# Two batches of a packed attention and FFN kernel: float32 products over half of d_ff in place of three float32r products

## The chip, the cores and the metric

The kernel runs on one core of a Trainium2 chip. The metric is the device time of one execution in microseconds; the median of three runs stands for a kernel. A profiled execution is a run of its own: it gives the span from the first to the last instruction, which is a little shorter than the device time.

## The reference

Two attentions follow one another, and an FFN follows them. With batch 8, 8 heads, 576 tokens, head size 64 and 32 packing vectors per head:

```python
p_packed = sm_attn(p, k, v)               # 32 packed vectors per head
out = sm_attn(q, p_packed, p_packed)      # 576 tokens attend to the 32
x = out.transpose(0, 2, 1, 3).reshape(B * S, H * D)      # 4608 x 512
h = x @ w_in                              # 512 -> 2048
g = np.maximum(h, 0.0) + alpha * np.minimum(h, 0.0)
return g @ w_out                          # 2048 -> 512
```

`sm_attn` is the softmax attention with scale 1/8. The weights w_in and w_out come to the kernel as 64-bit floating point numbers, which it converts itself on ACT and DVE.

## The kernel before

**The algebra.** The second attention's output is its probabilities a (576 tokens by 32 columns for each of 8 heads, 256 in all) times the packed vectors. The kernel multiplies the packed vectors into w_in first, giving pw (256 x 2048 for each batch, in pieces `pw[b, j]` of 512 columns of d_ff, j = 0 to 3). The FFN's first product is then pw against a, with a contraction of 256, two blocks of 128.

**Precision.** A float32 operand x is used either whole, as float32, or split into two float32r parts, xh = round(x) on ACT and xl = x - xh on DVE or POOL. A product of two split operands is three float32r products (hh, hl, lh). A product of two whole operands is one float32 product in the program, and two weight loads and two matmul records in the trace.

**The FFN loop.** The loop runs over 256 steps (k, f): k is a half-batch of 288 tokens (k // 2 is the batch), f one of 16 blocks of 128 of d_ff. At each step `first(k, f)` (L619) computes the first product into the PSUM tile `ps_h` (two buffers), then the activation: `neg` on ACT (L646) and a multiply and add on DVE back into `ps_h` (L647). Then the result is split: `gh` on ACT (L652), `gl` on DVE (L653). `second(k, f)` (L656), two steps behind, multiplies gh and gl by the f-th block of w_out into four accumulators `acc`, twelve float32r products a step (L670 to L672). The order of the steps is written out by hand: with `sweep(b, f0)` going over both half-batches of b, it is batch 0 f 0 to 3, batch 0 f 4 to 7, batch 1 f 0 to 7 (steps 0 to 31); batch 0 f 8 to 11, batch 0 f 12 to 15, batch 1 f 8 to 15 (steps 32 to 63); then batches 2 to 7 one after the other, 32 steps each. The accumulators hold one sweep; partial sums of the first two batches go through tiles `part`.

**First product.** For batch 0 (k < 2 * XF, XF = 1) it is whole: L628, two float32 products, with pw and a unsplit. For the others `split_pw` (L607) splits a piece of pw (256 columns of d_ff at a time: `pwh` on ACT for k < 4, L613, `pwl` on DVE, L616), and L640 to L642 are six float32r products a step.

**What feeds the loop.** Generators, each advanced once or more a step by a plan (L759 to L769) of (first step, generator, every how many steps; negative: how many times a step):

- `convert` (L106) turns a 512-column piece of 64-bit weights into float32 on ACT (L121, L123) and DVE (L125 to L139), and, if the caller wants it split, makes the parts on ACT (L141) and DVE (L142). `convert_w_out(f)` (L159) does this for the 16 blocks of w_out, two of them ahead of the loop, the next from step 0 on.
- `packed_w_fine` and `packed_w_first` make pw of batch 0 for j = 0 and 1 from whole w_in, and store the whole pieces in DRAM as `w_whole`.
- `packed_w` (L562) makes pw from split w_in. With "whole" it loads a piece of `w_whole` (256 KB, L572), splits it (ACT L573, DVE L574) and stores the parts as `w_split` (512 KB, L579); with "fresh" it converts from the input; otherwise it loads `w_split` (512 KB, L568). Three float32r products of 512 columns follow (L596 to L598), and ACT copies the result to pw (L601). Before, batch 1 takes j = 0 and 1 by "whole" from step 7, batches 0 and 1 take j = 2 and 3 by "fresh", and the later pairs load `w_split`, batches 2 and 3 from step 53.
- `attention(b, tp)` (L229) makes a of one batch for half of its heads in some 15 advances. Batches 0 and 1 use float32 products in it (`exact`), L207, L212 and L347; the others split. For batch 0 the end is one DVE transpose (L444) into a whole tile; for the others a transpose (L454), a cast on ACT to `a_h` (L455) and a subtraction on POOL to `a_l` (L456). The tiles `a_h` and `a_l` have three buffers each.

All DMAs go through SP's queue, in order. Within each engine the order of instructions is fixed when the program is built.

Of the kernel before, what the change touches and what calls it, by code (L numbers as in the profile page):

```python
# [8 lines left out]
F32 = mybir.dt.float32  # L9
# [13 lines left out]
def fv(ap):  # L23

    return ap.bitcast(F32)
# [3 lines left out]
def pack_attention_ffn_kernel(  # L29
# [74 lines left out]
    XF = 1  # L104

    def convert(src, raw, place, whole=None, room=None):  # L106
# [32 lines left out]
        nc.vector.tensor_tensor(out=bits, in0=bits, in1=low, op=ALU.add)  # L139
        hi, lo = place()  # L140
        nc.scalar.copy(out=hi, in_=mag)  # L141
        nc.vector.tensor_tensor(out=lo, in0=mag, in1=fv(hi), op=ALU.subtract)  # L142

# [15 lines left out]
    def convert_w_out(f):  # L159
        def place():  # L160
            wo_t[f] = const.tile([P, 2, DM], F32R, name=f"wo{f}", tag=f"wo{f}")
            return wo_t[f][:, 0, :], wo_t[f][:, 1, :]

        return convert(w_out[f * P : (f + 1) * P, :], new_raw(f), place)
# [64 lines left out]
    def attention(b, tp, exact=False):  # L229
# [211 lines left out]
        if b < XF:  # L441
            if b not in result:
                result[b] = at.tile([P, 2, S], F32, name="a_f", tag="a_h")
            nc.vector.transpose(  # L444
                out=result[b][:, tp, :], in_=t1.rearrange("p g n -> p (g n)")
# [3 lines left out]
            split_pt()  # L449
# [9 lines left out]


# [100 lines left out]

    def packed_w(bs, units, source="split"):  # L562
# [55 lines left out]

    def first(k, f):  # L619
# [4 lines left out]
        if k < 2 * XF:  # L624
            th, a_f = pw[k // 2, f // 4], result[k // 2]
# [20 lines left out]
        nc.scalar.activation(out=neg, in_=x, func=AF.Relu, scale=-1.0)  # L646
        nc.vector.scalar_tensor_tensor(  # L647
# [8 lines left out]
    def second(k, f):  # L656
# [10 lines left out]
        gh, gl = gs.pop((k, f))  # L667
        for o in range(NOC):
            os_ = slice(o * P, o * P + P)
            nc.tensor.matmul(acc[o][:, :HS], wo_t[f][:, 0, os_], gh, start=begin, stop=False)  # L670
            nc.tensor.matmul(acc[o][:, :HS], wo_t[f][:, 1, os_], gh, start=False, stop=False)  # L671
            nc.tensor.matmul(acc[o][:, :HS], wo_t[f][:, 0, os_], gl, start=False, stop=end)  # L672
# [16 lines left out]

    result, pw, pj, gs, acc, part = {}, {}, {}, {}, [], {}  # L690
# [20 lines left out]
    def units(*js):  # L711
        return [(j, pr) for j in js for pr in range(NP)]

# [51 lines left out]
    plan += [(A2[4], packed_w([2, 3], units(*range(NJ))), 1)]  # L765
# [51 lines left out]
```

## Time and profile before

| what | us |
|---|---|
| median of 3 runs | 811.91 (811.84 to 813.56) |
| profiled execution, span | 809.3 |
| PE, matmul records busy | 773.0 (5376 records) |
| PE, weight loads busy | 729.5 |
| DVE busy | 605.8 |
| ACT busy | 497.1 |
| POOL busy | 191.4 |
| mean granted TensorE clock | 0.992 |

Busy time is the union of an engine's records. A matmul's record goes on past the time in which the next one can start, so PE's busy time is above what its products need; the pace of a run of products in the chain of waits, or in a window that holds nothing else, says what one of them takes. In the groups a row gives the line, engine, operation, output and inputs, shapes and count, then busy time and mean duration of one in ns, then the idle time before it and what ended it. In the chain of waits a row has start, duration and what ran.

### The profile page before, as it was taken

Reading aid. Unit: us, or ns where it says so; the run is one execution under the profiler, and the core shown is the slowest. Engines: PE = TensorE matmul, PEld = TensorE weight load, DVE = VectorE, ACT = ScalarE, POOL = GpSimd, SP = SyncE. Lnnn points to the kernel's source line nnn. Section 1 sums busy time; section 2 is a strip of 40 time slices with the busy share of each in tenths; the row PEclk is TensorE's granted clock in tenths of the full one; section 3 lists DMA queues with packets and bytes.
Section 4 is the critical chain, followed back from the end, with each engine's and each line's share of the span. In section 5 each row is a group of like instructions: output and inputs, shape, how many; then the busy total and the mean of one; then the engine's idle time right before and its main releaser. Section 6 shows DMA issues by size and latency. Waiting matters only on the chain.

```text
span 809.3 us, 14930 instructions
## 1 busy us (share of the span) xinstructions
PE 773.0 (96%) x5376; PEld 729.5 (90%) x5376; DVE 605.8 (75%) x1301; ACT 497.1 (61%) x1165; POOL 191.4 (24%) x195
## 2 busy tenths in 40 slices
PE   6779899999989899999999999999999999999997
PEld 4557688989989799999999999999999999999997
DVE  3998989877887656898896477987875566666664
ACT  4888798876767775665657756665567533333332
POOL 2101411235346212354342014534410000000000
PEclk9979999999999999999999999999999999999999
DMA  9976787422223843322216722311027000000000
GB/s 312 340 233 223 262 304 236 151 54 83 78 88 101 267 151 104 93 59 82 70 59 212 235 59 59 91 58 45 2 92 256 20 31 1 31 1 31 1 30 30
DMA packets 58457, 93.77 MB, mean 116 GB/s; under 512 B 5136, under 2 KB 36880, under 8 KB 58384
## 3 DMA queue, kind: packets, MB, share of 16 engines
q1 hardware_dynamic: 58384, 92.83, 35.7%
q8 instruction: 42, 0.69, 0.4%
q14 instruction: 31, 0.25, 0.1%
HBM read 72.88 MB, written 19.92 MB: 115 GB/s over the span
## 4 chain that ended last, share of the span: by engine, by line
PE 80%; DVE 8%; DMA 5%; ACT 5%; issue 1%; POOL 0%; SPq 0%; ACTq 0%; DVEq 0%
PE acc L670 15%; PE acc L671 15%; PE acc L672 15%; PE ps_h L640 7%; PE ps_h L641 7%; PE ps_h L642 7%; PE ps_h L628 3%; DMA vraw<-in_v 2%; PE ps_m L352 2%; PE ps_m L216 1%; PE ps_m L217 1%; PE ps_m L596 1%; PE ps_m L598 1%; PE ps_m L597 1%; DMA w<-w_split 1%
## 5 line engine op out<-in xcount | busy, mean ns | idle before, releaser
L670 PE MATMUL acc<-gh,wo 128*128 128x288 f32 x1024 | 286.2, 300 | 3.5 <-ACT gh L652 3.1
L671 PE MATMUL acc<-gh,wo 128*128 128x288 f32 x1024 | 281.8, 295 | 0.0
L670 PEld LDWEIGHTS acc<-gh,wo 128*128 128x128 f32 x1024 | 192.2, 188 | 9.8 <-ACT gh L652 5.6
L672 PE MATMUL acc<-gl,wo 128*128 128x288 f32 x1024 | 199.2, 299 | 0.0
L671 PEld LDWEIGHTS acc<-gh,wo 128*128 128x128 f32 x1024 | 192.4, 188 | 1.6 <-issue 0.2
L652 ACT CAST gh<-ps_h 128x288 fp32r<-128x288 f32 x256 | 101.6, 399 | 115.3 <-DVE ps_h L647 113.2
L646 ACT ACTIVATE neg<-ps_h 128x288 f32<-128x288 f32 x256 | 105.3, 412 | 107.2 <-PE ps_h L642 95.5
L653 DVE TENSOR_TENSOR gl<-ps_h,gh 128x288 fp32r<-128x288 f32 x256 | 115.2, 452 | 70.4 <-ACT gh L652 68.5
L647 DVE SCALAR_TENSOR_TENSOR ps_h<-neg,nal,ps_h 128x288 f32<-128x288 f32 x256 | 131.2, 515 | 47.2 <-ACT neg L646 46.5
L672 PEld LDWEIGHTS acc<-gl,wo 128*128 128x128 f32 x1024 | 157.4, 188 | 3.1 <-issue 0.4
L640 PE MATMUL ps_h<-a_h,pwh 128*128 128x288 f32 x448 | 134.2, 300 | 4.1 <-DVE gl L653 4.0
L641 PE MATMUL ps_h<-a_l,pwh 128*128 128x288 f32 x448 | 132.3, 295 | 0.0
L642 PE MATMUL ps_h<-a_h,pwl 128*128 128x288 f32 x448 | 132.1, 295 | 0.0
L180 POOL TENSOR_TENSOR xl<-xraw,xh 128x576 fp32r<-128x576 f32 x48 | 71.4, 1488 | 175.2 <-ACT xh L179 171.1
L616 DVE TENSOR_TENSOR pwl<-pw,pwh 128x512 fp32r<-128x512 f32 x112 | 83.7, 748 | 9.1 <-ACT pwh L613 3.5
L640 PEld LDWEIGHTS ps_h<-a_h,pwh 128*128 128x128 f32 x448 | 84.2, 188 | 6.1 <-DVE gl L653 5.3
L641 PEld LDWEIGHTS ps_h<-a_l,pwh 128*128 128x128 f32 x448 | 84.3, 188 | 0.6
L642 PEld LDWEIGHTS ps_h<-a_h,pwl 128*128 128x128 f32 x448 | 84.1, 188 | 0.2
L601 ACT COPY pw<-ps_m 64x512 f32<-64x512 f32 x120 | 69.6, 580 | 15.2 <-PE ps_m L598 12.5
L615 DVE CAST pwh<-pw 128x512 fp32r<-128x512 f32 x96 | 52.0, 542 | 28.6 <-PE ps_h L641 27.8
L311 POOL TENSOR_TENSOR vs<-vraw,vs 128x640 fp32r<-128x640 f32 x24 | 40.4, 1682 | 51.3 <-ACT vs L310 50.3
L628 PE MATMUL ps_h<-a_f,pw 128*128 128x288 f32 x128 | 39.6, 433 | 3.8 <-DVE a_f L444 3.0
(127 smaller groups left out, 991.4 us busy)
## 6 DMA issues: line engine op xcount, KB each, us to landing
w<-w_split SPq DMA_DIRECT2D x48, 512.0 KB, 4.2
xraw<-in_kT SPq DMA_DIRECT2D x32, 288.0 KB, 2.9
xraw<-in_qT SPq DMA_DIRECT2D x32, 288.0 KB, 2.9
outT<-ot SPq DMA_DIRECT2D x64, 144.0 KB, 2.2
vraw<-in_v SPq DMA_DIRECT2D x32, 256.0 KB, 2.9
wraw<-in_w_in SPq DMA_DIRECT2D x16, 512.0 KB, 5.6
wraw<-in_w_out SPq DMA_DIRECT2D x16, 512.0 KB, 4.9
w_split<-w SPq DMA_DIRECT2D x16, 512.0 KB, 4.2
```

Source lines behind the costliest of these rows:

```text
L180: nc.gpsimd.tensor_tensor(out=xl, in0=raw, in1=fv(xh), op=ALU.subtract)
L616: nc.vector.tensor_tensor(out=tl, in0=src, in1=fv(th), op=ALU.subtract)
L640: nc.tensor.matmul(ps[:, :HS], th[:, i, fs], a_h[:, i, tok], start=hi, stop=False)
L641: nc.tensor.matmul(ps[:, :HS], th[:, i, fs], a_l[:, i, tok], start=False, stop=False)
L642: nc.tensor.matmul(ps[:, :HS], tl[:, i, fs], a_h[:, i, tok], start=False, stop=lo)
L646: nc.scalar.activation(out=neg, in_=x, func=AF.Relu, scale=-1.0)
L647: nc.vector.scalar_tensor_tensor(out=x, in0=neg, scalar=nal[:, f : f + 1], in1=x, op0=ALU.mult, op1=ALU.add)
L652: nc.scalar.copy(out=gh, in_=x)
L653: nc.vector.tensor_tensor(out=gl, in0=x, in1=fv(gh), op=ALU.subtract)
L670: nc.tensor.matmul(acc[o][:, :HS], wo_t[f][:, 0, os_], gh, start=begin, stop=False)
L671: nc.tensor.matmul(acc[o][:, :HS], wo_t[f][:, 1, os_], gh, start=False, stop=False)
L672: nc.tensor.matmul(acc[o][:, :HS], wo_t[f][:, 0, os_], gl, start=False, stop=end)
```

## The change

With WF = 8, for the first two batches (k < 4) and f < 8:

- the second product is one float32 product for each output block, from whole w_out and the whole activation g (written by DVE to SBUF; no gh, no gl);
- the first product is whole for batch 1 too (batch 0 is whole for all f, as before), from whole pw and whole a; batch 1's a is therefore made whole (`whole_a`) and split later, from step 36, for its other f;
- the split of w_out blocks 0 to 7, which later batches need, is put off to steps 33 to 40 (`split_steps`); until then whole blocks lie in tiles `wo_f` that share buffers with a_h and a_l;
- batch 1's pw for j = 0 and 1 is made by one float32 product from the loaded `w_whole` piece and whole packed vectors (`packed_w_one`), without splitting w_in. The splitting and storing of these eight pieces moves to batches 2 and 3, which now take j = 0 and 1 by "whole" from step 53.

```diff
+    WF = 8
+    wo_f, to_split = {}, []
...
+        if full is not None:
+            to_split.append((mag, place))
+            return
+        split_w(mag, place)
...
+    def split_steps():
+        while to_split:
+            split_w(*to_split.pop(0))
+            yield
...
+        def full():
+            if f % 2 == 0:
+                tag = "a_h" if f == WF - 2 else "a_l"
+                wo_f[f // 2] = at.tile([P, 2, DM], F32, name="wf", tag=tag)
+            return wo_f[f // 2][:, f % 2, :]
...
-        if b < XF:
+        if b < 2:
...
+    def split_a(b):
+        new_a(b)
+        a_h, a_l = result[b]
+        for tp in range(2):
+            nc.scalar.copy(out=a_h[:, tp, :], in_=whole_a[b][:, tp, :])
+            nc.gpsimd.tensor_tensor(
+                out=a_l[:, tp, :], in0=whole_a[b][:, tp, :], in1=fv(a_h[:, tp, :]),
+                op=ALU.subtract,
+            )
+            yield
...
+    def packed_w_one(b, units):
...
+            nc.tensor.matmul(ps[:64], ptf[:, pr, b], w, start=True, stop=True)
+            ro = (pr % 2) * 64
+            nc.scalar.copy(out=pw[b, j][ro : ro + 64, pr // 2, :], in_=ps[:64, :])
...
+    def whole_out(k, f):
+        return k < 4 and f < WF
+
+    def whole_in(k, f):
+        return k < 2 or whole_out(k, f)
...
-        if k < 2 * XF:
-            th, a_f = pw[k // 2, f // 4], result[k // 2]
+        if whole_in(k, f):
+            th, a_f = pw[k // 2, f // 4], whole_a[k // 2]
...
+        if whole_out(k, f):
+            g = gp.tile([P, HS], F32, name="g", tag="gh", bufs=3)
+            nc.vector.scalar_tensor_tensor(
+                out=g, in0=neg, scalar=nal[:, f : f + 1], in1=x, op0=ALU.mult, op1=ALU.add
+            )
+            gs[k, f] = g
+            return
...
+            if whole:
+                nc.tensor.matmul(
+                    acc[o][:, :HS], wo_f[f // 2][:, f % 2, os_], g, start=begin, stop=end
+                )
...
+    plan += [(33, split_steps(), 1), (36, split_a(1), 1)]
...
-    plan += [(PW1[0], packed_w([1], units(0, 1), "whole"), PW1[1])]
+    plan += [(PW1[0], packed_w_one(1, units(0, 1)), PW1[1])]
...
-    plan += [(A2[4], packed_w([2, 3], units(*range(NJ))), 1)]
+    plan += [(A2[4], chain(packed_w([2, 3], units(0, 1), "whole"), packed_w([2, 3], units(2, 3))), 1)]
```

More of the change, by code (lines that the diff above doesn't have):

```diff
@@ L104, in pack_attention_ffn_kernel, with convert @@
     XF = 1
-    def convert(src, raw, place, whole=None, room=None):
+    WF = 8
+    wo_f, to_split = {}, []
+    def convert(src, raw, place, whole=None, room=None, full=None):
         nc.sync.dma_start(out=raw if room is None else room, in_=src)
@@ L138, in convert, with split_w @@
             return
-        nc.vector.tensor_tensor(out=bits, in0=bits, in1=low, op=ALU.add)
+        if full is not None:
+            mag = full()
+        nc.vector.tensor_tensor(out=mag.bitcast(U32), in0=bits, in1=low, op=ALU.add)
+        if full is not None:
+            to_split.append((mag, place))
+            return
+        split_w(mag, place)
+    def split_w(mag, place):
         hi, lo = place()
@@ L162, in place @@
             return wo_t[f][:, 0, :], wo_t[f][:, 1, :]
-        return convert(w_out[f * P : (f + 1) * P, :], new_raw(f), place)
+        def full():
[3 more added lines that the diff above has]
+            return wo_f[f // 2][:, f % 2, :]
+        src = w_out[f * P : (f + 1) * P, :]
+        return convert(src, new_raw(f), place, full=full if f < WF else None)
     def load_x(src, b, pr):
@@ L440, in attention @@
         yield
-        if b < XF:
-            if b not in result:
-                result[b] = at.tile([P, 2, S], F32, name="a_f", tag="a_h")
+        if b < 2:
+            if b not in whole_a:
+                whole_a[b] = at.tile([P, 2, S], F32, name="a_f", tag="a_h")
             nc.vector.transpose(
-                out=result[b][:, tp, :], in_=t1.rearrange("p g n -> p (g n)")
+                out=whole_a[b][:, tp, :], in_=t1.rearrange("p g n -> p (g n)")
             )
@@ L448, in attention @@
             yield
-            split_pt()
+            if b == 0:
+                split_pt()
             return
@@ L560, in packed_w_first, with get @@
             yield
+    def packed_w_one(b, units):
+        def get(j, pr):
+            raw = xin.tile([P, 512], F32, name="w32", tag="xraw")
+            nc.sync.dma_start(out=raw, in_=w_whole[j, pr])
+            return raw
+        for got in ahead(get, units):
+            if got is None:
+                yield
+                continue
+            (j, pr), w = got
+            if pr == 0:
+                new_pw([b], j)
+            ps = ps_m.tile([P, 512], F32, name="ps_m", tag="m")
+            assert ("p", b, pr) in done
+            done.add(("w", b, j, pr))
+            nc.tensor.matmul(ps[:64], ptf[:, pr, b], w, start=True, stop=True)
+            ro = (pr % 2) * 64
+            nc.scalar.copy(out=pw[b, j][ro : ro + 64, pr // 2, :], in_=ps[:64, :])
+            yield
     def packed_w(bs, units, source="split"):
@@ L688, in second @@
                 nc.sync.dma_start(out=outT[o * P : (o + 1) * P, k * HS : k * HS + HS], in_=to)
+    whole_a = {}
     result, pw, pj, gs, acc, part = {}, {}, {}, {}, [], {}
@@ L712, in units, with chain @@
         return [(j, pr) for j in js for pr in range(NP)]
+    def chain(*gens):
+        for gen in gens:
+            yield from gen
     def drain(gen):
```

11 lines of the change are left out of this document (7 added, 4 removed).

## The prediction

> **What bounds the kernel now.** I read the page first, then the table of busy time by stage, then the chain of waits at three places, then TensorE's and the other engines' groups of one stage. A change in which 0.2% is lost or won is about what a measurement of this kernel can tell from no change; that is 1.6 us.
>
> The page gives the span, and a table by stage cuts it where the steps of the FFN loop do. Each step has one L646, and ACT's groups between 49 and 171 us, then between 171 and 277, hold 32 of them each: steps 0 to 31 (batches 0 and 1, f below 8), and steps 32 to 63 (the same batches, the other f).
>
> ```profile
> L646 ACT ACTIVATE neg<-ps_h 128x288 f32<-128x288 f32 x32 | 13.1, 412 | 3.1 <-PE ps_h L628 2.4 <-PE ps_h L642 0.6
> ```
>
> ```profile
> L646 ACT ACTIVATE neg<-ps_h 128x288 f32<-128x288 f32 x32 | 13.2, 412 | 9.6 <-PE ps_h L628 7.6 <-PE ps_h L642 1.8
> ```
>
> Columns of the stages: length, PE busy, weight load busy, DVE, ACT, POOL, PE clock, DMA share, GB/s.
>
> ```profile
> span 809.3 us, 14930 instructions
> ```
>
> ```profile
> 0.00:49.00 49.00, 31.34 (x142) 22.84 (x143) 35.09 (x84) 32.62 (x80) 7.82 (x27) 0.89 0.90 307
> 49.00:171.00 122.00, 116.39 (x696) 96.47 (x695) 109.30 (x224) 102.77 (x230) 27.38 (x26) 0.99 0.68 226
> 171.00:277.00 106.00, 101.89 (x695) 95.82 (x695) 83.88 (x194) 73.43 (x172) 46.69 (x45) 1.00 0.33 98
> 603.00:784.00 181.00, 181.00 (x1338) 179.13 (x1337) 111.28 (x228) 77.07 (x183) 2.59 (x2) 1.00 0.15 50
> ```
>
> In the stage 49 to 171, where nearly all of the change falls, DVE is busy 109.3 of 122 us (90%), ACT 102.8 (84%), PE 116.4 (95%). PE's figure is too high, since a matmul's record outlasts its place in the pipe. The rate must come from a stretch with nothing else in it. Here is one, and beside it rows of the chain at 195.3 (the four halves of two float32 products, then three float32r products, all 128x288) and at 76.7 (two float32 products of 288 columns, four float32r, then two float32 of 512).
>
> ```profile
> 700.00:750.00 50.00, 50.00 (x380) 50.00 (x378) 32.02 (x66) 17.27 (x44) 0.00 (x0) 1.00 0.04 13
> ```
>
> ```profile
> 195.28 0.97 PE ps_h L628 x4
> 196.25 0.40 PE acc L672 x3
> ```
>
> ```profile
> 76.70 0.97 PE ps_h L628 x4
> 77.68 0.53 PE acc L672 x4
> 78.21 1.72 PE ps_m L486 x4
> ```
>
> 380 float32r products in 50 us are 0.1316 us each, three of them 0.395. A float32 product shows as two records and takes 0.97/2 = 0.485. So one float32 product costs PE 0.09 more than the three it replaces: the change makes PE slower, and can pay only where PE waits for DVE and ACT. For that I count what PE really streams in 49 to 171, from its groups there.
>
> ```profile
> L670 PE MATMUL acc<-gh,wo 128*128 128x288 f32 x124 | 36.3, 311 | 2.1 <-ACT gh L652 1.8 <-ACT part L676 0.3
> L628 PE MATMUL ps_h<-a_f,pw 128*128 128x288 f32 x63 | 19.8, 435 | 0.6 <-DVE gl L653 0.6
> L640 PE MATMUL ps_h<-a_h,pwh 128*128 128x288 f32 x32 | 9.7, 303 | 1.0 <-DVE gl L653 1.0
> L596 PE MATMUL ps_m<-w,pt 128*64 128x512 f32 (+1 forms) x16 | 6.9, 428 | 0.3 <-ACT w L141 0.2
> L347 PE MATMUL ps_m<-vraw,aT 128*64 128x128 f32 x40 | 6.0, 306 | 0.0
> L212 PE MATMUL ps_m<-xraw,ptf 128*64 128x288 f32 x16 | 5.2, 425 | 1.6 <-ACT ptf L383 1.6
> L216 PE MATMUL ps_m<-xh,s 128*128 128x288 f32 x8 | 2.5, 317 | 0.0
> ```
>
> L671 and L672 repeat L670's count, L641 and L642 that of L640, L217 that of L216: 3x124 + 3x32 + 2x8 = 484 products of 288 columns at 0.1316 are 63.7 us. L628's 63 halves and the 24 halves at L212 (8 of them beside the 16 shown), at 0.2425, are 21.1. L596 to L598 are 48 products of 512 columns, 0.1316x512/288 = 0.234 each: 11.2. Eight halves at L486 (1.72/4) are 3.4. The 40 at L347 and some 29 small ones, at about 0.11 (an estimate: 0.2425x128/288), are 7.6. Sum: **107 us of 122; PE stands still for 15 us** in all. That is the whole prize in this stage, however much DVE and ACT are relieved. The same count for 171 to 277:
>
> ```profile
> L670 PE MATMUL acc<-gh,wo 128*128 128x288 f32 x132 | 36.8, 299 | 0.6 <-ACT gh L652 0.6
> L628 PE MATMUL ps_h<-a_f,pw 128*128 128x288 f32 x60 | 17.2, 409 | 0.1
> L640 PE MATMUL ps_h<-a_h,pwh 128*128 128x288 f32 x36 | 11.0, 306 | 2.0 <-DVE gl L653 2.0
> L216 PE MATMUL ps_m<-xh,p 128*128 128x288 f32 x16 | 5.0, 323 | 0.0
> L352 PE MATMUL ps_m<-vs,aT 128*128 128x256 f32 x30 | 4.6, 285 | 0.2 <-DVE s_t L220 0.2
> L596 PE MATMUL ps_m<-w,pt 128*128 128x512 f32 x7 | 2.9, 417 | 0.7 <-DMA w<-w_split 0.7
> ```
>
> With L216 and L217 at 24 each (8 more of another tile), 553 products of 288 columns are 72.8, L628 14.5, L596 to L598 4.9, L352 3.5 (256 columns) and 31 small ones some 2.5: 98 of 106, so about 7% standstill.
>
> **The change part by part.**
>
> *PE.* The second product over f below 8 for four half-batches: 32 steps x 4 output blocks = 128 products, each three float32r before, one float32 after: 128 x 0.09 = +11.5 us. The first product of batch 1 over f below 8: 16 steps x 2 = 32 products, +2.9. Batch 1's w_in products for j = 0 and 1: eight of 512 columns, 0.86 against 3x0.234 = 0.70: +1.3. Sum **+15.7 us on PE**, all in the stage 49 to 171: 107 + 15.7 = 122.7, which is already the stage's present length. The Trainium skill (FP8 and Floating Point Precision, section TensorE Precision Notes) says that true FP32 takes four passes through the array. Four passes at this trace's 0.1316 would be 0.526 a product and +21 us instead of +14.4 for the 160 products of 288 columns; the chain's 0.485 lies below that, and I use the row.
>
> *DVE and ACT, relieved.* Their groups in 49 to 171 (L142's other group there is that of w, which stays):
>
> ```profile
> L653 DVE TENSOR_TENSOR gl<-ps_h,gh 128x288 fp32r<-128x288 f32 x31 | 13.8, 452 | 5.2 <-ACT gh L652 4.9
> L616 DVE TENSOR_TENSOR pwl<-pw,pwh 128x512 fp32r<-128x512 f32 x10 | 7.3, 742 | 2.3 <-ACT pwh L613 2.3
> L142 DVE TENSOR_TENSOR wo<-mag,wo 128x512 fp32r<-128x512 f32 x10 | 6.8, 685 | 0.4 <-ACT wo L141 0.3
> L574 DVE TENSOR_TENSOR w<-w,w 128x512 fp32r<-128x512 f32 x8 | 6.4, 800 | 1.8 <-ACT w L573 1.7
> ```
>
> ```profile
> L652 ACT CAST gh<-ps_h 128x288 fp32r<-128x288 f32 x32 | 12.5, 398 | 2.5 <-DVE ps_h L647 2.2
> L141 ACT CAST wo<-mag 128x512 fp32r<-128x512 f32 x10 | 6.2, 621 | 0.3 <-DVE mag L139 0.3
> L613 ACT CAST pwh<-pw 128x512 fp32r<-128x512 f32 x10 | 6.1, 620 | 1.5 <-PE ps_h L641 1.5
> L573 ACT CAST w<-w 128x512 fp32r<-128x512 f32 x8 | 5.0, 619 | 2.1 <-DMA w<-w_whole 2.1
> ```
>
> Gone for good: 32 gl (14.5 us) and 8 pwl (5.9) on DVE; 32 gh (12.7) and 8 pwh (5.0) on ACT. Moved behind step 33: the splits of eight w_out blocks, 0.685 on DVE and 0.62 on ACT each; about four of them lie before 49 (below). Moved behind step 53: eight splits of w_in, 6.4 and 5.0. So the stage loses 14.5 + 5.9 + 2.7 + 6.4 = 29.5 us of DVE work and about 25 of ACT's: DVE falls from 109 to 80, ACT from 103 to 78, both about 63% of some 128 us. Both stop setting the pace. The chain from a first product to its second also loses the gh and gl steps (0.40 + 0.45), and ps_h comes free after the L647 step.
>
> *What is left of PE's 15 us.* Bounds: nothing regained (stage 122 + 15.7), or all (122.7). Between them the rows to go by are 603 to 784, where DVE is busy 61% and ACT 43% (1338 records at 0.1316 are 176 of 181 us, under 3% of standstill), and the stage itself with 12%. I take 5%, nearer the former because the loads are like it, but not on it, because attention and the conversion of w_in are still threaded through and the clock is still low at its start (0.99 over the stage). 122.7/0.95 = 129.1: **+7.1 us**.
>
> *Before 49.* Steps 0 and 1 of w_out are converted before the loop and run ahead. The DVE groups up to 49 hold four such splits, and the chain there runs through DVE into the first FFN product:
>
> ```profile
> L142 DVE TENSOR_TENSOR wo<-mag,wo 128x512 fp32r<-128x512 f32 x4 | 2.7, 672 | 0.0
> ```
>
> ```profile
> 44.54 0.56 DVE wo L142
> 45.10 0.67 DVE t L439
> ```
>
> All four lie ahead of the first product in a crowded DVE queue. Gain between 0 (other work takes the place) and 2.7; I take **-2**, as the row with the wait of L439 behind L142 shows one of them directly on the chain.
>
> *Later stages.* The stage 171 to 277 has DVE at 83.9 of 106 (79%). It receives the eight w_out splits (5.5) and most of the w_in splits (6.4): 95.8, or 90%. The splits of batch 1's a move to one ACT cast and one POOL subtraction for each half, POOL being busy 46.7 of 106. Queued behind these on DVE and ACT are neg, L647, gh and gl, for which PE waits. At 90% the stage 49 to 171 had 12% of PE standstill; at 79% this one has 7%. Zero to +4; I take **+1**, since the steps 33 to 53 leave room to spread them. The tiles of whole w_out and whole a share three buffers each with a_h and a_l, so batch 2's a waits for a buffer until about step 42; it is due at step 64, some 60 us later, so this costs nothing.
>
> The sum is 15.7 on PE, less 8.6 of standstill, less 2, plus 1: +6.1, so 809.3 + 6.1 = 815.4 for the profiled execution. The median before is 811.9, 2.6 above the span; I carry that over: **818 us**.
>
> **The rivals.**
>
> *PE has more room than I count (faster).* What decides is whether the loop's standstill is all DVE's and ACT's lateness. If the stages 49 to 277 run as tightly as 603 to 784 (about 2%), the first takes 122.7/0.98 = 125.2 (+3.2), the second regains about 5 of its 7 (-5), and 2.7 is saved before 49: 807.5 in the metric. The Trainium skill (Perfetto Trace Analysis, section Identifying the Most-Contended Engine) would have headroom judged by the share of weight loading, not by matmul time. Weight loading is 96.5 of 122 us here; by it 25 us are free, PE would swallow all 15.7, and the stage could fall below 122, to perhaps 112 and the time to 800. Against it: in the row of 700 to 750, weight loading does read 50.00 of 50, but the 0.97 us of the two float32 products hold less than that, four loads with the mean below, 0.78 of 0.97, so a stage full of float32 looks open by that measure when it is not.
>
> ```profile
> L628 PEld LDWEIGHTS ps_h<-a_f,pw 128*128 128x128 f32 x128 | 22.9, 196 | 11.8 <-DVE a_f L444 3.2 <-DVE gl L653 1.9 <-issue 0.8
> ```
>
> *It balances (no change).* The standstill in 49 to 171 falls to about 3% (+4.5), 2.7 is saved before 49 and nothing is lost later: 813.7, at the edge; with a little more regained, 812.
>
> *Batches 2 and 3 get their w_in late (slower still).* Their first eight units now load 256 KB, split, and write 512 KB, where they loaded 512 KB. In the chain these loads already end two waits:
>
> ```profile
> 270.73 4.31 DMA w<-w_split
> 276.14 5.74 DMA w<-w_split
> ```
>
> With 256 KB more a unit at the 226 GB/s that the stage 49 to 171 sustained, that is 1.1 us a unit, 9 us over eight, beside ACT and DVE splits of 1.4 us in a row for each. It decides if the fourth unit lands after step 64 wants it: then up to +9 comes on top, 827. For it: the two waits. Against it: the load itself is halved, the write is waited for only through a buffer, and the plan starts these units at step 53.
>
> **How the numbers follow.** My forecast (slower by 2 to 11) gets 0.58, the late w_in 0.12, PE with room 0.17, the balance 0.13. The likeliest is 818. The range reaches down into PE with room, to 808.5, and up to the middle of the late w_in, 825. Faster by over 0.2% 0.17, within 0.2% 0.13, slower 0.70.
>
> **What would show it.** Right: in the profile after, steps 16 to 32 pass no faster than before, the second product's float32 pairs stand back to back at 0.97 for two, DVE and ACT fall to about 63% in the stage, and step 32 comes some 5 us later than 171. The first step comes 1 to 2.7 us earlier. Wrong: step 32 arrives before 171 (PE had room), or float32 products in the second product cost other than 0.485, or the chain at steps 60 to 72 goes through w_whole, L573 and L574 (late w_in).

## The result, and the profile after

The changed kernel takes 851.57 us (median of four runs, 850.01 to 853.42), the kernel before 812.73 (four runs, 811.84 to 815.29). The ratio is 1.047, 95% interval 1.045 to 1.050: 38.8 us slower, where some 6 were forecast (818) and the range ended at 825.

From the page of the changed kernel: the span, and in the groups the two kinds of float32 product. The second row is the TensorE clock in 40 slices of 21.2 us.

```profile
span 848.0 us, 14519 instructions
PEclk9969899999989999999999999999999999999999
L690 PE MATMUL ps_h<-a_f,pw 128*128 128x288 f32 x192 | 58.9, 431 | 13.8 <-DVE a_f L466 11.0
L741 PE MATMUL acc<-g,wf 128*128 128x288 f32 x256 | 67.7, 408 | 0.1
```

256 records at L741 are the 128 second products, two records each; the 192 at L690 are 96 first products, 64 of batch 0 and 32 of batch 1. The clock row has three weak slices here: the third, the fifth and the twelfth. Before, only the third is below 9.

The stages of the changed kernel, cut near the same steps as the prediction's rows. A step begins with its `neg` on ACT: step 0 at 53.4 us, step 32 at 190.3, step 64 at 309.0 (the rows are cut some half a us later); before they were 49.1, 171.1 and 277.3. The columns are length, then busy time of PE, weight loading, DVE, ACT and POOL with the instructions, granted clock, DMA share, GB/s:

```profile
0.00:54.00 54.00, 30.37 (x141) 22.42 (x142) 40.38 (x93) 34.94 (x85) 8.37 (x27) 0.87 0.89 301
54.00:191.00 137.00, 131.52 (x518) 90.59 (x516) 82.95 (x161) 77.62 (x167) 18.43 (x21) 0.95 0.44 146
191.00:310.00 119.00, 109.63 (x709) 100.26 (x708) 94.10 (x209) 82.81 (x191) 49.06 (x48) 0.97 0.35 111
310.00:848.00 538.00, 523.54 (x3844) 513.80 (x3844) 378.91 (x801) 288.77 (x684) 110.17 (x100) 1.00 0.24 79
...
135.90:190.80 54.90, 54.86 (x237) 43.41 (x236) 29.79 (x59) 32.56 (x67) 9.16 (x7) 1.00 0.29 100
...
217.50:251.50 34.00, 29.01 (x180) 27.06 (x179) 25.64 (x61) 20.98 (x50) 15.96 (x15) 0.90 0.27 80
```

DVE and ACT did fall in the second row, from 109 and 103 to 83 and 78. The stage got longer all the same, and so did the next.

Where the 38.7 us of span went. PE's work in a stretch is its matmul records counted by form, each form at its full-clock pace (0.1316 for a float32r product of 288 columns, 0.242 for half of a float32 one, other widths in proportion); standstill is the rest of the stretch, lost clock included.

| stretch | before | after | longer by | of it PE work | of it standstill |
|---|---|---|---|---|---|
| to step 0 | 49.1 | 53.4 | 4.3 | | 4.3 |
| steps 0 to 31 | 122.0 | 136.9 | 14.9 | 12.1 | 2.8 |
| steps 32 to 63 | 106.2 | 118.7 | 12.5 | 3.9 | 8.7 |
| the rest | 532.0 | 539.0 | 7.0 | | 7.0 |

PE work rose by 16.0, against 15.7 in the forecast; some attention products slid from the first half to the second, which is why the second has a share. The other 22.7 is standstill that was not there before. Cut finer, it rose by 4.8 in steps 0 to 8, 3.2 in 8 to 16, 7.5 in 40 to 48, 4.9 in 64 to 80 and some 4 in 128 to 192. It fell by 5.2 in steps 16 to 32, where the row at 135.90 shows PE busy for 54.86 of 54.90 us, and by some 2 in steps 80 to 96. Part of it is lost clock: in steps 0 to 16 the granted clock is 0.92 over 82.0 us, where it was 0.98 over 70.0, so some 5 of the 8.0 us there are clock (an estimate: 0.08 x 82.0 less 0.02 x 70.0).

Three places can be read directly. The first is the start. DVE's timeline of the changed kernel (start, duration):

```profile
27.33 0.68 DVE L152 TENSOR_TENSOR wo<-wf,wo 128x512 fp32r<-128x512 f32 x1
...
43.02 0.68 DVE L143 CUSTOM_DVE_ANT_0 wf<-mag,low 128x1024 uint16<-128x1024 uint16 x1
...
46.74 0.62 DVE L152 TENSOR_TENSOR wo<-wf,wo 128x512 fp32r<-128x512 f32 x1
...
49.28 0.68 DVE L143 CUSTOM_DVE_ANT_0 wf<-mag,low 128x1024 uint16<-128x1024 uint16 x1
50.56 0.75 DVE L466 STREAM_TRANSPOSE a_f<-t 128x576 f32<-128x576 f32 x1
...
66.55 0.69 DVE L152 TENSOR_TENSOR wo<-wf,wo 128x512 fp32r<-128x512 f32 x1
```

In the kernel before, the same transpose, which completes batch 0's a, lies here:

```profile
46.95 0.77 DVE L444 STREAM_TRANSPOSE a_f<-t 128x576 f32<-128x576 f32 x1
```

It comes 3.6 us later, behind conversions of w_out. And the splits that the plan holds back until step 33 (L152 into `wo` from `wf`) were not held back: they run between 27 and 67 us. The plan's step is not when an engine does the work; the order of an engine's queue is. That order is not simply the order in which the plan issues: the program is built with `schedule_with_timeline_sim=True`, and here splits stand ahead of step 0 that the plan issues at step 33. By what rule the builder places them, no run shows.

The second place is the clock. PE's waits of the changed kernel in 40 to 110 us (total, times, longest), and then the chain of waits where two long ones end:

```profile
PE ps_h L690 <- DVE a_f L466: 11.0, 2, 8.6
PE ps_m L369 <- ACT pw L522: 2.4, 1, 2.4
```

```profile
50.64 0.69 DVE a_f L466
...
51.37 2.29 PE ps_h L690 x4
...
58.89 1.94 PE acc L741 x8
60.83 0.97 PE ps_h L690 x4
...
239.07 0.63 ACT wo L151
239.70 0.04 issue
239.74 1.33 PE acc L746 x4
...
242.62 0.24 PE acc L747
...
245.11 0.13 PE acc L747
...
296.27 0.63 ACT w L629
...
298.52 0.58 ACT pw L657
299.13 0.38 ACT w L629
...
303.00 0.62 ACT w L629
...
306.61 0.62 ACT w L629
307.26 0.58 ACT pw L657
```

After the wait that ends at 51.3, four records of float32 take 2.29 us, and 0.97 nine us later. After the one at 239.7 a float32r product takes 0.24, and 0.13 from 245 on. The third place is 296 to 311, around step 64: the chain runs for most of that time on ACT, through the copies of new pieces of pw (L657) and, between them, the splits of w_in (L629) that the change moved there. It is the smallest of the three: standstill in steps 56 to 64 rose by 1.3.

### The profile page after: what moved, and what is told of

Same layout as the page of the kernel before. It is cut to its first block, busy times and chain, and to the rows that moved or that the text cites. A ratio compares the mean times of both kernels' runs of the same rounds, so it can differ in the third digit from the quotient of the medians.

```text
span 848.0 us, 14519 instructions
## 1 busy us (share of the span) xinstructions
PE 795.1 (94%) x5208; PEld 727.1 (86%) x5208; DVE 596.3 (70%) x1261; ACT 484.1 (57%) x1125; POOL 186.0 (22%) x195
## 3 DMA queue, kind: packets, MB, share of 16 engines
q1 hardware_dynamic: 58384, 90.73, 32.7%
## 4 chain that ended last, share of the span: by engine, by line
PE 77%; DVE 8%; ACT 5%; DMA 2%; issue 1%; POOL 0%; ACTq 0%; DVEq 0%
PE acc L746 13%; PE acc L747 13%; PE acc L748 12%; PE acc L741 7%; PE ps_h L702 6%; PE ps_h L703 6%; PE ps_h L704 6%; PE ps_h L690 5%; ACT pw L657 1%; PE ps_m L374 1%; PE ps_m L652 1%; DVE pwl L672 1%; PE ps_m L654 1%; PE ps_m L653 1%; PE ps_m L238 1%
## 5 line engine op out<-in xcount | busy, mean ns | idle before, releaser
L746 PE MATMUL acc<-gh,wo 128*128 128x288 f32 x896 | 250.1, 299 | 11.6 <-ACT gh L721 6.0
L747 PE MATMUL acc<-gh,wo 128*128 128x288 f32 x896 | 248.3, 296 | 0.0
L746 PEld LDWEIGHTS acc<-gh,wo 128*128 128x128 f32 x896 | 168.5, 188 | 16.1 <-ACT gh L721 8.7
L748 PE MATMUL acc<-gl,wo 128*128 128x288 f32 x896 | 175.8, 297 | 0.0
L747 PEld LDWEIGHTS acc<-gh,wo 128*128 128x128 f32 x896 | 168.9, 189 | 0.9
L721 ACT CAST gh<-ps_h 128x288 fp32r<-128x288 f32 x224 | 89.4, 400 | 122.8 <-DVE ps_h L716 117.6
L722 DVE TENSOR_TENSOR gl<-ps_h,gh 128x288 fp32r<-128x288 f32 x224 | 100.9, 453 | 69.4 <-ACT gh L721 67.5
L716 DVE SCALAR_TENSOR_TENSOR ps_h<-neg,nal,ps_h 128x288 f32<-128x288 f32 x224 | 114.7, 515 | 43.4 <-ACT neg L708 42.8
L748 PEld LDWEIGHTS acc<-gl,wo 128*128 128x128 f32 x896 | 138.8, 188 | 1.7 <-DVE gl L722 0.2
L702 PE MATMUL ps_h<-a_h,pwh 128*128 128x288 f32 x416 | 123.9, 298 | 1.3 <-DVE pwh L671 0.6
L657 ACT COPY pw<-ps_m 64x512 f32<-64x512 f32 x112 | 65.1, 582 | 18.7 <-PE ps_m L654 15.2
L690 PE MATMUL ps_h<-a_f,pw 128*128 128x288 f32 x192 | 58.9, 431 | 13.8 <-DVE a_f L466 11.0
L741 PE MATMUL acc<-g,wf 128*128 128x288 f32 x256 | 67.7, 408 | 0.1
```

The lines of the kernel that those rows point to most:

```text
L690: nc.tensor.matmul(ps[:, :HS], th[:, i, fs], a_f[:, i, tok], start=(i == 0), stop=(i == 1))
L702: nc.tensor.matmul(ps[:, :HS], th[:, i, fs], a_h[:, i, tok], start=hi, stop=False)
L716: nc.vector.scalar_tensor_tensor(out=x, in0=neg, scalar=nal[:, f : f + 1], in1=x, op0=ALU.mult, op1=ALU.add)
L721: nc.scalar.copy(out=gh, in_=x)
L722: nc.vector.tensor_tensor(out=gl, in0=x, in1=fv(gh), op=ALU.subtract)
L741: nc.tensor.matmul(acc[o][:, :HS], wo_f[f // 2][:, f % 2, os_], g, start=begin, stop=end)
```

## The experiments

The theory: the float32 price on PE is as forecast, and the rest is the order of the engines' queues. That order is fixed when the program is built, and the change moved conversions, splits and loads in it, so that PE waits in new places. The rivals: float32 products cost PE more than counted; w_in for batches 2 and 3 comes late; the attention of batches 2 and 3, from its first scores to its last packed vectors, starts too late and paces step 64 (supply). All kernels were timed in three rounds beside the kernel before; differences are of medians taken together on one chip. Line numbers in rows of an experiment are its own. Edits are against the changed kernel unless said otherwise; `...` stands for lines between.

**1. One part at a time.** First, without the whole w_in products (they are split again, at their old places):

```diff
-    plan += [(PW1[0], packed_w_one(1, units(0, 1)), PW1[1])]
+    plan += [(PW1[0], packed_w([1], units(0, 1), "whole"), PW1[1])]
...
-    plan += [(A2[4], chain(packed_w([2, 3], units(0, 1), "whole"), packed_w([2, 3], units(2, 3))), 1)]
+    plan += [(A2[4], packed_w([2, 3], units(*range(NJ))), 1)]
```

> The changed kernel with batch 1's w_in products put back: three float32r products from split w_in for j = 0 and 1, split and stored in the first stage, so that batches 2 and 3 load the stored parts. Both FFN products over f below 8 stay whole. TensorE's price falls by 1.3 us against the changed kernel. Theory spread (each part of the change disturbs the fixed order a little, each adds its own standstill): 835 to 845. Theory loads (the excess is the late w_in: loads that keep their buffer until TensorE's product, and stores that hold SP's queue): 827 to 832. Theory early (the excess is made in the first 60 us by conversions of whole w_out blocks that run ahead of batch 0's a, and the half clock after it): stays above 845.

Second, the whole second product alone (f below 6), with the edit above and

```diff
-    WF = 8
+    WF = 6
...
-        if b < 2:
+        if b < 1:
...
-        return k < 2 or whole_out(k, f)
+        return k < 2
...
-    plan += [(33, split_steps(), 1), (36, split_a(1), 1)]
+    plan += [(33, split_steps(), 1)]
```

> The kernel before with only the second product whole, for f below 6 (f below 8 doesn't fit its buffers alone): 96 products, +8.6 us of TensorE work. First products, batch 1's a and w_in as before. Theory spread: 822 to 830. Theory loads: 817 to 822 (only the price of the products, less a little). Theory early: 830 or more, with the second transpose into batch 0's a some 4 us later than before's 46.9 us.

Third, batch 1's whole first product alone, again with the first edit and

```diff
-    WF = 8
+    WF = 0
...
-        return k < 2 or whole_out(k, f)
+        return k < 2 or (k < 4 and f < 8)
...
-    plan += [(33, split_steps(), 1), (36, split_a(1), 1)]
+    plan += [(36, split_a(1), 1)]
```

> The kernel before with only batch 1's first product over f below 8 whole, from whole a that is split later; w_out, the second product and w_in as before: +2.9 us of TensorE work. Theory spread: 815 to 822. Theories loads and early: 812 to 816.

Fourth, the whole w_in products and the splits that move with them, and nothing else:

```diff
-    WF = 8
+    WF = 0
...
-        if b < 2:
+        if b < 1:
...
-        return k < 2 or whole_out(k, f)
+        return k < 2
...
-    plan += [(33, split_steps(), 1), (36, split_a(1), 1)]
```

> The kernel before with only batch 1's w_in products whole, and the splitting and storing of the eight pieces moved to batches 2 and 3: +1.3 us of TensorE work. Theory spread: 815 to 822. Theory loads: 828 or more. Theory early: 812 to 816.

| kernel | ratio to before (95%) | us | PE price by count | left |
|---|---|---|---|---|
| without whole w_in | 1.028 (1.025 to 1.031) | +22.2 | 14.4 | 7.8 |
| second product alone, f < 6 | 1.024 (1.022 to 1.027) | +19.1 | 8.6 | 10.5 |
| first product alone | 1.009 (1.006 to 1.012) | +8.3 | 2.9 | 5.4 |
| w_in alone | 1.023 (1.020 to 1.026) | +18.0 | 1.3 | 16.7 |

The price is the prediction's 0.09 us a product, for 160, 96 and 32 products, and its 1.3 for w_in. The part with the least of it leaves the most over. The first and the fourth kernel hold the whole change between them, and their 22.2 and 18.0 come to 40.2, against 38.8. The second and third don't add up to the first (27.4, with 2.9 of PE work less), so what is left over is not a sum of parts. One thing is not told apart in these two: their plan has one entry more than before, so from step 33 or 36 on the entries behind it change sides of the first product. Of the three theories in the expectations each foresaw one kernel's time (spread the first, early the second, loads the fourth), and none the third's 823.3.

In the fourth kernel's trace the excess lies in steps 8 to 32 (8.6 us longer than before), 48 to 56 (4.9), 64 to 80 (9.7) and 128 to 192 (4.0); the moved splits begin at step 53. Among the waits of SP's queue, which issues all loads, in 50 to 120 us two are of a kind that the kernel before can't have (total, times, longest):

```profile
SPq L600 <- PE ps_m L613: 9.7, 5, 4.0
SPq L195 <- PE ps_m L613: 5.1, 3, 3.3
```

L600 is the load of whole w_in into the buffers in which attention's q and k arrive (L195). A load there waits until PE has read the one before (L613), and the loads queued behind it wait too. Before, the whole pieces were loaded into these buffers as well, but the split on ACT and DVE gave them free, not a product on PE.

**2. The buffers of whole w_in.** The same loads go into the buffers of split w_in:

```diff
     def get(j, pr):
-            raw = xin.tile([P, 512], F32, name="w32", tag="xraw")
+            raw = new_w32()
```

> The changed kernel with batch 1's whole w_in pieces loaded into the three buffers of split w, not into the three that attention's q and k use. Theory buffer: q and k loads, and all behind them in SP's queue, no longer wait for TensorE's w_in products (21 us of such waits in steps 0 to 16); steps 0 to 16 fall by 5 us or more, time 840 to 846. Rival (the order of TensorE's queue, not the buffers, makes batch 1's a late): 849 to 853.

Measured 1.043 (1.040 to 1.047), +36.0: lower by some 3 us, with intervals that overlap. Steps 0 to 16 of the changed kernel, and then of this one:

```profile
53.90:135.90 82.00, 76.56 (x280) 47.09 (x279) 53.06 (x103) 45.16 (x100) 9.27 (x14) 0.92 0.55 177
...
54.50:129.70 75.20, 73.15 (x283) 45.74 (x282) 48.27 (x95) 43.20 (x97) 9.41 (x14) 0.97 0.53 168
```

They are 6.8 us shorter. Some 4 of that is clock, 0.97 in place of 0.92 (an estimate: 0.08 x 82.0 less 0.03 x 75.2); what is left for the waits on SP is under 3, and experiment 3 regains nearly as much in these steps with the buffers unchanged. So the buffers are one way into this loss, not shown to be its cause. Most of it is gone again at the end: step 48 is reached at 243.5 against 251.1, but the trace ends only 1.1 us earlier.

**3. The splits and stores of w_in put back in the first stage.** The eight pieces are also split and stored where they are loaded, and batches 2 and 3 load them split:

```diff
+            w = win.tile([P, 2, 512], F32R, name="w", tag="w")
+            nc.scalar.copy(out=w[:, 0, :], in_=raw)
+            nc.vector.tensor_tensor(
+                out=w[:, 1, :], in0=raw, in1=fv(w[:, 0, :]), op=ALU.subtract
+            )
+            nc.sync.dma_start(out=w_split[j, pr], in_=fv(w))
...
-    plan += [(A2[4], chain(packed_w([2, 3], units(0, 1), "whole"), packed_w([2, 3], units(2, 3))), 1)]
+    plan += [(A2[4], packed_w([2, 3], units(*range(NJ))), 1)]
```

> The changed kernel with the eight pieces of w_in also split and stored in the first stage, as before, beside their whole products; batches 2 and 3 load the stored parts. ACT and DVE have 5.0 and 6.4 us more to do in the first stage and less later. Theory moved splits: steps 48 to 56 and 64 to 80 regain their 7 to 9 us, steps 0 to 16 lose 0 to 4: time 842 to 847. Rival (the whole products themselves disturb): 850 or more.

Measured 1.036 (1.033 to 1.039), +29.8: 9.0 less than the changed kernel; the profiled execution is 5.0 shorter (843.0 against 848.0). That is the time that the expectation named, but not its mechanism. Where the moved splits are gone, little changes: steps 48 to 56 take 25.7 us (25.2 in the changed kernel), 56 to 64 take 33.9 (32.7), and 64 to 80 fall from 53.4 to 51.5. Steps 0 to 16, where this kernel has the splits in addition, fall from 82.0 to 76.6. So the size of the late w_in (up to 9) is met by luck; the gain lies elsewhere.

**4. The start.** A whole block of w_out is made in the ring tile `mag` as before, ACT copies it to its own tile, and it is split at once:

```diff
+        nc.vector.tensor_tensor(out=bits, in0=bits, in1=low, op=ALU.add)
         if full is not None:
-            mag = full()
-        nc.vector.tensor_tensor(out=mag.bitcast(U32), in0=bits, in1=low, op=ALU.add)
-        if full is not None:
-            to_split.append((mag, place))
-            return
+            nc.scalar.copy(out=full(), in_=mag)
```

> The changed kernel with whole w_out blocks made as before, in the three-buffer tile in which the split is made too, and then copied by ACT (0.6 us for each of eight) into their own tile. Theory ring: whole blocks written straight to their own tile free the ring early, so conversions are queued ahead of batch 0's a, and the first step comes 4.8 us late with the clock at half behind it. Then the first step starts near 49 to 51 us again and the time is 838 to 846. Rival: the start is late for another reason (the whole tiles themselves, the second product): first step still near 54, time 849 to 856 with the added copies.

Its timeline has the transpose of a in its old place:

```profile
45.87 0.77 DVE L463 STREAM_TRANSPOSE a_f<-t 128x576 f32<-128x576 f32 x1
```

Step 0 begins at 48.1 us instead of 53.4. The time is 1.050 (1.048 to 1.052), +41.1, no better: the 5 us are lost again between steps 64 and 96, which take 107.2 us in place of 98.4. That it is the ring was put to the test from the other side. This kernel is the kernel before with blocks 0 to 7 of w_out made in tiles of their own and split at once; all products are as before, so PE's work is the same:

```diff
+    wo_f = {}
...
-        nc.vector.tensor_tensor(out=bits, in0=bits, in1=low, op=ALU.add)
+        if full is not None:
+            mag = full()
+        nc.vector.tensor_tensor(out=mag.bitcast(U32), in0=bits, in1=low, op=ALU.add)
...
-        return convert(w_out[f * P : (f + 1) * P, :], new_raw(f), place)
+        return convert(src, new_raw(f), place, full=full if f < 8 else None)
```

> The kernel before with w_out blocks 0 to 7 made whole in tiles of their own, as in the change, and split from there at once; both products stay split, so TensorE's work is that of before. Theory order: first step at 53 to 55 us, the clock at half for 13 us, and 5 to 20 us slower in all, 818 to 835. Rival (the whole products bring the standstill): first step late but the time within 5 us of before.

```profile
51.16 0.77 DVE L454 STREAM_TRANSPOSE a_f<-t 128x576 f32<-128x576 f32 x1
```

Measured 1.014 (1.010 to 1.019), +12.0, and step 0 at 54.8. So where the block is written, without one float32 product, makes the late start; the buffers that the new tiles share with a_h and a_l don't, as the kernel with the ring tile has those too. Why it does is inferred: a block in its own tile gives its ring tile back earlier, the next conversion is ready earlier, and stands ahead of the attention in DVE's queue.

**5. The wait at 239 us.** PE waits there for the cast of block 15 of w_out. First, one more block is converted for each three steps instead of four; second, blocks 14 and 15 are made right behind 13:

```diff
-    WO, W1, AT1 = (-7, 5, 4), 2, (-1, 2, -3)
+    WO, W1, AT1 = (-7, 5, 3), 2, (-1, 2, -3)
```

> The changed kernel with one number of the plan changed: from the fifth on, a w_out block is converted every 3 steps, not every 4, so that block 15 is asked for at step 31, not 40. Theory late block: the 4 us wait for block 15's cast and the 6.8 us of half clock behind it go, steps 40 to 48 fall from 34 to about 26 us, time 841 to 845. Rival (DVE is full there whatever the order): the standstill only moves, time 848 to 853.

```diff
-            if i + 1 >= n:
+            if i + 1 >= n and i < 11:
```

> The changed kernel with w_out blocks 14 and 15 converted one step after block 13 (steps 33 and 34, not 36 and 40), the others as they were. Theory late block: the wait for its cast and the half clock behind it go, 8 us less in steps 40 to 48. If that is all that bounds there: 841 to 846. If it is given back before step 64, as with a block every 3 steps: 848 to 856.

The first kernel's steps 40 to 48 and 56 to 64:

```profile
211.50:235.00 23.50, 23.41 (x157) 21.71 (x156) 16.92 (x41) 13.45 (x33) 10.51 (x11) 1.00 0.29 87
258.50:307.00 48.50, 39.80 (x230) 33.48 (x228) 36.59 (x78) 31.92 (x71) 19.91 (x21) 0.86 0.48 157
```

Steps 40 to 48 fall from 34.0 us (the row at 217.50 above) to 23.5, with PE busy throughout and the clock at 1.00. Then steps 56 to 64, 32.7 us in the changed kernel, take 48.5 at clock 0.86. In all 1.055 (1.052 to 1.059), +44.8, above what either side of the expectation allowed. The second kernel's steps 40 to 48:

```profile
219.00:244.60 25.60, 24.87 (x163) 22.59 (x161) 20.60 (x50) 16.29 (x40) 13.26 (x13) 1.00 0.32 94
```

8.4 us better there, and 1.044 (1.040 to 1.049), +35.9, in all: about 3 kept at most, as the intervals overlap.

**6. Supply.** If the attention of batches 2 and 3 paced step 64, starting it earlier should help. The changed kernel, and then the kernel before, with the same one line:

```diff
-    A2 = (24, 29, 34, 38, 53)
+    A2 = (18, 23, 28, 33, 50)
```

> The changed kernel with the plan's steps for attention of batches 2 and 3 moved up from 24, 29, 34, 38 to 18, 23, 28, 33, and their w_in products from 53 to 50. In the eight kernels run so far step 64 follows the last packed vectors of batch 3 by 17 to 24 us, and these follow batch 2's first scores by 117 to 132 us. Theory supply (from step 32 on this chain of attention sets the pace, and it starts late because its start hangs on a step number): first scores come some 15 us earlier, step 64 at 295 to 302 in place of 309.5, time 837 to 845. Rival pace (the chain runs slower because the loop does, its start is no matter): step 64 stays within 3 us of 309.5, time 847 to 855.

> The kernel before with the same earlier attention steps, as a control. Theory supply: there the loop itself leaves TensorE only 7 us of standstill between steps 32 and 64, so at most some 5 us are to be won: 808 to 815. Rival pace: within 1.5 us of before or slower.

The changed kernel takes 1.052 (1.047 to 1.056), +42.6. The attention did come earlier: batch 2's first scores (L238) at 133.2 us in place of 165.1, the last packed vectors of batch 3 (L398) at 272.1 in place of 282.1. Step 64 came later all the same, at 320.7 in place of 309.0, so the supply theory falls. The other side of the expectation, that step 64 stays, is missed too. The kernel before, its instructions the same in kind and number and only five numbers of the plan different, takes 1.025 (1.023 to 1.027), +20.9. Its first two FFN stages:

```profile
48.50:183.00 134.50, 121.93 (x725) 101.91 (x723) 110.01 (x227) 106.16 (x240) 29.70 (x30) 0.98 0.62 208
183.00:297.50 114.50, 102.32 (x657) 95.14 (x658) 84.22 (x184) 76.71 (x173) 43.95 (x41) 0.96 0.39 122
```

134.5 and 114.5 against 122.0 and 106.2: nearly all of the loss is there. Order alone can cost 21 us. PE's longest wait in 205 to 250 us is one that the changed kernel has too, for the cast of block 15 of w_out (its L151), with half the clock behind it (0.24 us a float32r product until 242):

```profile
PE acc L670 <- ACT wo L141: 5.0, 1, 5.0
```

That not every touch of the order costs is shown by two empty entries in the plan of the kernel before:

```diff
+    plan += [(33, iter(()), 1), (36, iter(()), 1)]
```

> The kernel before with two empty entries in the plan at steps 33 and 36, as the change adds them: no instruction more or less, but the entries behind them swap sides of the first product for three steps. Theory order (any change of issue order in the first 64 steps costs standstill): 816 to 830. Rival (only large moves cost): within 1.6 us of before.

Measured 0.999 (0.997 to 1.001), -0.3. The entries behind the new ones change sides of the first product for three steps, and that costs nothing: the theory in its strict form, that any change of order in the first 64 steps costs standstill, is wrong. It takes larger moves.

**7. The price on PE by itself.** The ring kernel of experiment 4 with the same tiles and the same order, but each whole second product as one float32r product of rounded w_out and g, which leaves out the two correction products:

```diff
-                wo_f[f // 2] = at.tile([P, 2, DM], F32, name="wf", tag=tag)
+                wo_f[f // 2] = at.tile([P, 2, DM], F32R, name="wf", tag=tag)
...
-            g = gp.tile([P, HS], F32, name="g", tag="gh", bufs=3)
+            g = gp.tile([P, HS], F32R, name="g", tag="gh", bufs=3)
```

> As the kernel with whole blocks made through the ring and copied (854.9), but the second product over f below 8 for the first two batches is a single float32r product of rounded w_out and rounded g, so it leaves out the two correction terms; DVE's and ACT's work is the same. It takes 128 x 0.353 = 45 us off TensorE. If TensorE's price is what costs: 810 to 825. If the loop after step 32 hangs on attention's chain that starts by step number: the first stage shrinks by 30 us or more but 5 to 15 us are given back before step 64, 820 to 835. If the price doesn't matter at all: 845 to 855.

It takes 813.85 us, 0.999 (0.997 to 1.001), -1.3 against before, and 42.4 less than the ring kernel (differences to before of -1.3 and +41.1). By count, 128 products at 0.485 less 0.1316 are 45.2. The price is paid almost one for one. The stages:

```profile
50.00:148.00 98.00, 89.48 (x390) 58.95 (x389) 83.64 (x165) 79.72 (x172) 16.95 (x19) 0.96 0.65 209
148.00:266.50 118.50, 109.17 (x710) 99.98 (x708) 95.26 (x211) 83.18 (x194) 50.09 (x49) 0.97 0.36 112
```

This kernel's PE has 45.2 less 15.7, some 29.5 us, less to do than before, and only just equals it. So it has about 28 us more standstill than the kernel before, with DVE at 85% in the first row and the second stage as long as in the changed kernel. How much of that is order and how much the pace of DVE and ACT, now that PE has less to do, is not told apart.

**8. Repairs joined.** The ring tile of experiment 4, the faster blocks of 5, the early stores of 3 and the early attention of 6 together:

> The changed kernel with four things at once: whole blocks made through the ring and copied, a w_out block every 3 steps, the eight w_in pieces split and stored in the first stage, attention of batches 2 and 3 earlier. Theory supply: with the chain early the gains of the first three are no longer given back, and the 15.4 us of TensorE's price with 4 to 10 us of standstill is left: 826 to 838. Rival pace: 842 to 856. None of the theories has it under before's 812.

Measured 1.034 (1.030 to 1.037), +27.0: 11.8 better than the changed kernel, though of the four parts only the stores had gained by themselves (9.0), and the others had lost 2.3, 6.0 and 3.8 (of these only the 6.0 is clear of noise). Repairs of an order don't add up either. Then the three that had kept something or cured a place, without the two that had not: no whole w_in (experiment 1), the ring tile, and block 15 right behind 13:

> The changed kernel without whole w_in products (as e1, 837), with whole blocks made through the ring and copied, and block 15 early. If the gains add up: 822 to 829. If they are given back: 834 to 842. Slower than before either way.

```profile
PEclk9879999999999999999999999999999999999999
...
48.00:176.00 128.00, 124.37 (x525) 90.02 (x525) 90.30 (x177) 87.55 (x185) 18.41 (x21) 0.99 0.63 208
176.00:291.50 115.50, 106.69 (x706) 97.57 (x704) 88.77 (x198) 76.27 (x180) 52.42 (x49) 1.00 0.32 97
```

Measured 1.019 (1.015 to 1.024), +16.4. The clock row has no weak slice behind the third, and step 0 begins at 48.0 us. Its PE work is 14.4 above before by count, so only 2 us of standstill are left over, where the changed kernel has 22.7: the w_in part, the tile in which whole blocks are made and the late block 15 hold nearly all of it between them. This is the best that the change came to with both FFN products whole, without its w_in part, and it is still slower than the kernel before; none of these kernels is faster than that beyond the noise.

## Why the prediction was wrong

The sum was 15.7 on PE, less 8.6 of standstill in the first stage, less 2 before it, plus 1 behind it. The price came as forecast. The three terms of standstill, -9.6 together, are what failed: measured they are +22.7.

*The price on PE: right.* 15.7 forecast, 16.0 counted, though 3.9 of it fell behind step 32, as attention products slid there. The chain above gives 1.94 for eight records (four products) at L741 and 0.97 for two at L690. The Trainium skill (FP8 and Floating Point Precision, section TensorE Precision Notes) counts four passes for true FP32, from which four times this trace's 0.1316, an estimate, would be 0.526 for a product; the trace says 0.485 in the second product as in the first. And the experiment with one pass shows that PE's price goes into the time.

*DVE and ACT relieved: right.* Forecast 80 and 78 in the stage, measured 82.95 and 77.62.

*"Steps 16 to 32 pass no faster than before": right.* 54.9 us against 52.0, and no standstill.

*"What is left of PE's 15 us": -8.6, measured +2.8.* The prediction took 5% of standstill for the first stage, "nearer the former because the loads are like it". The former was a late stage in which no attention and no conversion runs any more. In the changed kernel standstill in the stage is 18.4 of 136.9, not 6.4 of 129.1. It fell where the argument fits (steps 16 to 32) and rose by 8.0 in steps 0 to 16, some 5 of it lost clock. Step 32 came 19.2 us later, not some 5. The relief itself is real: without the whole w_in products (first kernel of experiment 1) the stage takes 126.7 us, with their loads in other buffers (experiment 2) 129.3, with the last three repairs joined 128.0, near the forecast's 129.1. Counted in the same way, standstill is then 9.6 to 10.9 us, some 5 below the 15.9 of before; that the lengths agree so well is partly luck, as PE's work in the stage is 117 to 118 us there, not the forecast's 122.7. So the stage's term failed on what the change put in the way in steps 0 to 16, which the busy shares of DVE and ACT don't tell. In the last of these kernels about as much is lost again in steps 32 to 63, which take 115.2 against 106.2.

*"Before 49": -2, measured +4.3.* The prediction took the plan's step 33 for the time of the splits. They ran from 27 us on, and the conversions came ahead of batch 0's a (experiment 4).

*"Later stages": +1, measured +15.7,* the largest miss (8.7 of standstill in steps 32 to 63 and 7.0 behind). DVE reached 94.1 us in that stage, as forecast (95.8), but the stage grew, and DVE was at 79% of it. In steps 40 to 48, which hold 7.5 of it, what was late was a single instruction, the cast of block 15: brought forward it leaves PE busy there (experiment 5). Most of that gain was then lost again, so the rest of the term is not traced to one place.

*Tiles shared with a_h and a_l at no cost:* nothing in the waits speaks against it. *Loads that hold the buffers of q and k until PE's product:* not costed at all; with other buffers steps 0 to 16 are 6.8 us shorter, some 4 of it by the clock (experiment 2).

*The rivals.* PE with room (0.17) was wrong, and so was the reading by weight loading: it is 43.41 of 54.90 us in steps 16 to 32, while PE has nothing free. The late w_in (0.12) had a size of up to 9, and its sign is there: the chain at 296 to 311 goes through those splits. But taking the splits away leaves steps 56 to 64 no shorter (experiment 3), and by itself it would have given 827. No case had the loss of order in it, which is larger than the price of the products.

*What stays open.* Why the whole w_in products alone cost 16.7 us beyond PE's price: the places are known (experiment 1), the cause is not, and no run shows whether half of it is the moved splits. What holds steps 56 to 64 in the first kernel of experiment 5, beyond the low clock there. Where the 4 us in steps 128 to 192 come from, which most of these kernels lose. And by what the order of a queue could be foreseen from the plan: nearly every local repair was given back further on, in part or whole, and no run shows by what rule.

## What to carry to other kernels

Where a kernel threads several chains through in-order queues, cost an edit in two parts: what it adds to the bounding engine, which can be counted and will be paid, and what it moves in the queues, which cannot be read from busy shares. Relieving DVE and ACT, 84% to 90% busy, did regain some 5 of PE's 16 us of standstill here, but only in kernels where something else that the change had moved was put back or given room; look at which single instruction ends each long wait before counting on more. And measure how much the order alone is worth first, by moving one number of the plan with the instructions unchanged: if that is worth 20 us, a gain of 5 from fewer instructions can't be told in advance.

## What the runs showed of the hardware

A wait of PE costs more than itself. The one of 3.9 us that ends at 239.7 is followed by products at 0.24 us, half the pace, until about 245, and the 8.6 us wait before step 0 by float32 records at half the pace to about 57. The mean granted clock fell from 0.992 to 0.980: 0.020 of 848.0 us less 0.008 of 809.3 is 10.5 us of full clock, an upper bound of what this cost, as PE would not have been busy in all of it. The Trainium skill (TensorE: Matmul & The Clock Gate, Part 1) has the clock halve after an idle window of some 3.4 us and come back after a busy one of the same length, the windows running free of the program. These two places agree with it. The third weak stretch, some 98 to 108 (the fifth slice of the clock row), does not quite: the wait before it is only 2.4 us long (L369 in the list above), and it is followed by ten us at half pace with shorter waits in between. The same section puts the cost of the warm-up ramp below 1% of a typical span. The 0.8% of clock lost in the kernel before agrees; the 2.0% here come from low stretches after waits in the middle of the kernel.
